# The residual add of block 11 as an accumulating DMA on the GpSimd queue, in a cross-network kernel with a full TensorE

## Chip, cores, metric

One core of one Trainium2 chip. The metric is device time in microseconds. All runs quoted are marked fast, and repeated runs of the kernel before agree within 0.1%.

## The reference

Six layers of a "deep cross network" on 16384 rows of 1024 columns, in bf16:

```python
# x0: (16384, 1024), ws: (6, 1024, 1024), bs: (6, 1024)
x = x0
for l in range(6):
    proj = jnp.einsum('bd,de->be', x, ws[l]) + bs[l]
    x = x0 * proj + x
return x
```

## The kernel before

The batch is cut into 16 pairs of 2 x 512 rows; a pair goes through its six layers before the next starts. x lives in SBUF transposed, as four quadrants (half of the columns, half of the rows). The 2 x 2 block product is done with seven products instead of eight (sums T1 to T4 of x quadrants against precombined weights), and in pairs 1 to 15 two of the seven (5 and 2) are cut once more in the same way. The result of the blocks comes out of PSUM through ScalarE into Q (block 11), U, V, W; VectorE then adds the shared part, multiplies by x0 and adds into x. In pair 0 the kernel also makes the precombined weights; 36 copies on GpSimd's DMA queue store them in HBM (`Lc`), and these are the "GpSimd copies" of the prediction.

Every operation is put into a list with a rank, and a small list scheduler emits them in the order of rank as soon as their tags allow; the order on each engine is therefore fixed when the kernel is built. The parts that matter here (`#...` marks cuts):

```python
# weights: a ring of 16 buffers; SyncE loads ahead as far as TensorE has freed buffers
def pump():
    while pos["next"] < len(ring_seq):
        u, w, kind = ring_seq[pos["next"]]
        #...
        nc.sync.dma_start(t[:], w_src(units[u][1], w))
        pos["next"] += 1

# ranks of a middle layer, in microseconds from its start (cut)
#   5cc@10.88 T3@11.48 2cc@12.61 Q1@13.35 Qm@14.62 Qa@15.89 Ua@17.43 ... T1@-1.14

B11, B12, B21, B22 = blk(xs, 0, 0), blk(xs, 0, 1), blk(xs, 1, 0), blk(xs, 1, 1)
ttop("T1", T[1][:], B12, B11, SUB, [XI[0, 1], XI[0, 0]], ["T1"])      # first reader of the new x11
ttop("T2", T[2][:], B22, T[1][:], SUB, [XI[1, 1], "T1"], ["T2"])
ttop("T3", T[3][:], B22, B12, SUB, [XI[1, 1], XI[0, 1]], ["T3"])
#...
group(f"P1.{m}", "1", pA[m], A[m], B11, [XI[0, 0]], m, True)          # first matmuls that read x11
#...
ttop("Q1", Q[:], Q[:], P1s[:], ADD, allm("Q") + allm("P1s"), allm("Q"))
for nm, C, q in (("Q", Q, (0, 0)), ("U", U, (0, 1)), ("V", V, (1, 1)), ("W", W, (1, 0))):
    #...
    ttop(nm + "m", C[:], C[:], blk(x0T, *q), MULT, ...)               # Qm, Um, Vm
    ttop(nm + ("a" if nm == "Q" else "x"), blk(xst, *q), C[:], blk(xs, *q), ADD, ...)  # Qa, Ux, Vx, Wx
#...
if l == (2 if pr == 0 else 0) and nxt < NPAIR:                        # next pair's x0, transposed on load
    #...
        op(base + 23 + n, ld, [], XN)
```

## Time and profile before

| | before |
|---|---|
| time | 2276.61 us (2276.53 to 2276.68) |
| TensorE / VectorE / ScalarE / GpSimd busy | 100% / 91% / 81% / 1% |
| one layer of pairs 1 to 15 | 23.45 us |
| DMA engines: SyncE's queue / GpSimd's queue | 79.1% / 2.2% of 16 engines |

Busy shares say how full an engine is, not whether it holds up the end. That is read from the chain that ended last and from who waits for whom; both are in the prediction. In the lines of a timeline the columns are start, duration, engine, source line, operation, written tile <- read tiles, shapes, count; a bracket gives the idle time just before and what ended it. `ev` are the buffers Q, U, V, W; `T` the sums T1 to T4; `ti` the inputs of the inner products; `xst` is x. "Landing" is the time from the start of a DMA's issuing instruction to the moment when its data is reported as written. The DMA share adds up the times of all packets and divides by the time of 16 engines; packets overlap, so it can exceed 1.

### The profile page before, as it was taken

Reading aid. Unit: us, or ns where it says so; the run is one execution under the profiler, and the core shown is the slowest. Engines: PE = TensorE matmul, PEld = TensorE weight load, DVE = VectorE, ACT = ScalarE, POOL = GpSimd, SP = SyncE. Lnnn points to the kernel's source line nnn. Section 1 sums busy time; section 2 is a strip of 40 time slices with the busy share of each in tenths; the row PEclk is TensorE's granted clock in tenths of the full one; section 3 lists DMA queues with packets and bytes.
Section 4 is the critical chain, followed back from the end, with each engine's and each line's share of the span. In section 5 each row is a group of like instructions: output and inputs, shape, how many; then the busy total and the mean of one; then the engine's idle time right before and its main releaser. Section 6 shows DMA issues by size and latency. Waiting matters only on the chain.

```text
span 2275.2 us, 34978 instructions
## 1 busy us (share of the span) xinstructions
PE 2265.4 (100%) x12951; PEld 1264.0 (56%) x12951; DVE 2079.9 (91%) x2326; ACT 1839.4 (81%) x3228; POOL 22.1 (1%) x43
## 2 busy tenths in 40 slices
PE   9999999999999999999999999999999999999998
PEld 4455555555555555555555555555555555555554
DVE  7999999999999999999999999999999999999997
ACT  5678888888888888888888888888888888888887
POOL 1110000000000000000000000000000000000000
PEclk9999999999999999999999999999999999999999
DMA  9779797796977969779697796978969689696872
GB/s 279 229 270 289 261 242 269 219 301 209 252 257 221 288 217 260 250 226 283 213 274 241 228 283 204 273 245 230 283 200 292 226 232 286 194 303 216 241 240 65
DMA packets 625868, 557.01 MB, mean 245 GB/s; under 512 B 397600, under 2 KB 552224, under 8 KB 625696
## 3 DMA queue, kind: packets, MB, share of 16 engines
q1 hardware_dynamic: 618864, 534.58, 79.1%
q0 software_dynamic: 5184, 18.88, 2.2%
q8 instruction: 101, 1.65, 0.3%
q10 hardware_dynamic: 1648, 1.32, 0.2%
q14 instruction: 71, 0.58, 0.1%
HBM read 436.22 MB, written 52.43 MB: 215 GB/s over the span
## 4 chain that ended last, share of the span: by engine, by line
PE 98%; DVE 1%; SPq 0%; DMA 0%; issue 0%; ACT 0%; DVEq 0%
PE pA L285 57%; PE pX L389 24%; PE pX L285 16%; DVE ev L198 1%; SPq L529 0%; DMA wp<-in_ws_dram 0%; DVE xst L198 0%; DVE T L198 0%; DVE ti L198 0%; DVE wp L198 0%; SPq L538 0%; ACT ev L294 0%; DVE x0T L487 0%; DVEq L608 0%; DVEq L198 0%
## 5 line engine op out<-in xcount | busy, mean ns | idle before, releaser
L285 PEld LDWEIGHTS <-wp 128*128 128x128 bf16 x7904 | 772.3, 98 | 843.7 <-issue 3.9
L285 PE MATMUL pA<-T,wp 128*128 128x512 bf16 x4608 | 1054.9, 379 | 0.5 <-DVE T L198 0.5
L294 ACT ACTIVATE ev<-pA,b_all 128x512 bf16<-128x512 f32 x1124 | 704.8, 690 | 211.8 <-PE pA L285 211.4
L389 PEld LDWEIGHTS <-wp 128*128 128x128 bf16 x4984 | 487.1, 98 | 156.6 <-issue 15.2
L198 DVE TENSOR_TENSOR ev<-ev,x0T 128x2048 bf16<-128x2048 bf16 (+2 forms) x484 | 482.7, 999 | 8.1 <-ACT ev L294 1.5
L198 DVE TENSOR_TENSOR xst<-ev,xst 128x2048 bf16<-128x2048 bf16 x319 | 388.9, 1219 | 18.6 <-DVE ev L198 0.5
L389 PE MATMUL pX<-ti,wp 128*128 128x256 bf16 x2848 | 397.6, 272 | 0.0
L198 DVE TENSOR_TENSOR ev<-ev,ev 128x2048 bf16<-128x2048 bf16 (+1 forms) x283 | 343.7, 1215 | 26.7 <-ACT ev L294 9.8
L294 ACT ACTIVATE ev<-pX,b_all 128x512 bf16<-128x512 f32 x412 | 289.4, 705 | 59.9 <-PE pX L285 49.3
L285 PE MATMUL pX<-xst,wp 128*128 128x512 bf16 x1376 | 336.4, 379 | 0.0
L285 PE MATMUL pA<-xst,wp 128*128 128x512 bf16 x1280 | 313.5, 379 | 0.0
L290 ACT COPY pX<-pA 128x512 f32<-128x512 f32 x412 | 256.3, 625 | 44.7 <-PE pA L285 44.3
L290 ACT CAST ev<-pX 128x512 bf16<-128x512 f32 x384 | 224.8, 619 | 49.0 <-ACT ev L294 37.6
L198 DVE TENSOR_TENSOR ev<-iu,ip 128x1024 bf16<-128x1024 bf16 x178 | 122.4, 688 | 120.7 <-ACT iu L290 120.7
L290 ACT COPY pX<-pX 128x512 f32<-128x512 f32 x356 | 208.7, 587 | 8.4
L290 ACT CAST iu<-pX 128x512 bf16<-128x512 f32 x356 | 196.8, 639 | 0.0
L198 DVE TENSOR_TENSOR T<-xst 128x2048 bf16<-128x2048 bf16 x160 | 194.8, 1217 | 0.3
L198 DVE TENSOR_TENSOR T<-xst,T 128x2048 bf16<-128x2048 bf16 x160 | 194.5, 1216 | 0.0
L389 PE MATMUL pX<-T,wp 128*128 128x256 bf16 x1068 | 160.2, 273 | 0.0
L290 ACT CAST ip<-pX 128x512 bf16<-128x512 f32 x178 | 104.7, 589 | 54.1 <-PE pX L389 54.1
L389 PE MATMUL pX<-xst,wp 128*128 128x256 bf16 x888 | 133.2, 273 | 0.0
L198 DVE TENSOR_TENSOR xst<-ev,x0T 128x2048 bf16<-128x2048 bf16 x64 | 78.2, 1222 | 1.6
(44 smaller groups left out, 624.3 us busy)
## 6 DMA issues: line engine op xcount, KB each, us to landing
wp<-Lc SPq DMA_DIRECT2D x538, 512.0 KB, 4.6
wp<-in_ws_dram SPq DMA_DIRECT2D x285, 512.0 KB, 5.3
out_dram<-x0T SPq DMA_DIRECT2D x30, 1024.0 KB, 8.6
Lc<-wp POOLq DMA_DIRECT2D x24, 512.0 KB, 6.2
Lc<-isum POOLq DMA_DIRECT2D x12, 512.0 KB, 6.9
w<-in_ws_dram SPq DMA_DIRECT2D x5, 512.0 KB, 6.3
wp<-in_ws_dram ACTq DMA_DIRECT2D x2, 512.0 KB, 5.8
out_dram<-x0T SPq DMA_DIRECT2D x2, 512.0 KB, 3.6
```

Of the source, the lines that this page charges most:

```text
L198: nc.vector.tensor_tensor(out=o, in0=a, in1=b, op=op)
L285: nc.tensor.matmul(bank[:], lhsT=wt[(u, w)][:, k, m * P:(m + 1) * P], rhs=rhs[:, k, :], start=(start and k == 0), stop=(k == KH - 1), skip ...
L290: add(name, lambda: nc.scalar.copy(out=dst, in_=src), rd, wr)
L294: add(name, lambda: nc.scalar.activation(out=dst, in_=src, func=IDENT, bias=b_all[:, c:c + 1], scale=1.0), rd, wr)
L389: nc.tensor.matmul(pX[bank][:, m * NQ:(m + 1) * NQ], lhsT=wv[:, k, m * P:(m + 1) * P], rhs=rhs[:, k, :], start=(start and m == 0 and k == ...
```

## The change

VectorE is the second fullest engine and GpSimd does nothing after pair 0. The intent is to take one of VectorE's large adds away: from layer 1 of pair 1 on (in layer 0 the sum is written to another buffer, so there is nothing to accumulate into), Q is added into x by a DMA that reads Q and x and writes x.

```diff
                     ttop(nm + "m", C[:], C[:], blk(x0T, *q), MULT, allm(nm) + [X0[q]], allm(nm))
+                if nm == "Q" and l > 0 and not one:
+                    add("Qa", lambda C=C, q=q, xst=xst: nc.gpsimd.dma_start(out=blk(xst, *q), in_=C[:], accum_op=ADD), allm(nm) + [XI[q]], [XO[q]])
+                    continue
                 ttop(nm + ("a" if nm == "Q" else "x"), blk(xst, *q), C[:], blk(xs, *q), ADD, allm(nm) + [XI[q]], [XO[q]])
```

## The prediction

> **What bounds the kernel now.** I read the page from the top: busy shares, chain, DMA queues, then the timeline of two engines in a middle layer, then the DMA load of four stretches.
>
> ```profile
> PE 2265.4 (100%) x12951; PEld 1264.0 (56%) x12951; DVE 2079.9 (91%) x2326; ACT 1839.4 (81%) x3228; POOL 22.1 (1%) x43
> q1 hardware_dynamic: 618864, 534.58, 79.1%
> q0 software_dynamic: 5184, 18.88, 2.2%
> PE 98%; DVE 1%; SPq 0%; DMA 0%; issue 0%; ACT 0%; DVEq 0%
> L198 DVE TENSOR_TENSOR xst<-ev,xst 128x2048 bf16<-128x2048 bf16 x319 | 388.9, 1219 | 18.6 <-DVE ev L198 0.5
> ```
>
> TensorE never stops: 100% busy at a granted clock of 0.999, and 98% of the chain that ended last is TensorE. VectorE is second at 91%, but TensorE's waits for it are fractions of a microsecond in the whole run. So taking work off VectorE cannot shorten anything; the change can only be neutral or put a new wait in front of TensorE. The question is whether the add, done by DMA, is ready when it is needed. The block-11 product Q, the sum into x, and the next user of x stand so in a middle layer (VectorE first, TensorE after; the eleven matmul lines between are left out):
>
> ```profile
> 1060.83 1.22 DVE L198 TENSOR_TENSOR ev<-ev,x0T 128x2048 bf16<-128x2048 bf16 x1
> 1062.15 1.23 DVE L198 TENSOR_TENSOR xst<-ev,xst 128x2048 bf16<-128x2048 bf16 x1
> 1063.46 1.23 DVE L198 TENSOR_TENSOR ev<-ev,ev 128x2048 bf16<-128x2048 bf16 x1
> ...
> 1068.26 1.22 DVE L198 TENSOR_TENSOR T<-xst 128x2048 bf16<-128x2048 bf16 x1
> 1069.40 0.68 DVE L198 TENSOR_TENSOR ev<-ev,x0T 128x1024 bf16<-128x1024 bf16 x1
> 1070.00 0.68 DVE L198 TENSOR_TENSOR ti<-T 128x1024 bf16<-128x1024 bf16 x1
> ...
> 1069.45 1.89 PE L285 MATMUL pA<-xst,wp 128*128 128x512 bf16 x8
> 1071.17 0.60 PE L389 MATMUL pX<-ti,wp 128*128 128x256 bf16 x4
> ```
>
> The first line is the multiplication by x0 (Qm), the second the add that the change removes (Qa), the third the next block's first add (Ua), then T1 = B12 - B11, the first reader of the new x; the first two TensorE groups of the next layer read x and then a product of T1.
>
> **The window.** Qm ends at 1060.83 + 1.22 = 1062.05. T1 starts at 1068.26: 6.2 us later. Beyond that there is almost no slack. From T1 on VectorE works without a gap, and T2 = B22 - T1 ends just in time: in the layer before, T2 ran from 1052.96 to 1054.18 and its matmuls began at 1054.26, 0.08 us later. The inner-product input made from T1 ends at 1070.68, its matmuls start at 1071.17, 0.5 us later. So the DMA is free if it lands within about 6.3 us of Qm's end; each microsecond beyond delays T1, T2 and TensorE, and through TensorE the next layer's Q. TensorE has no idle time in which to make it good. The layer is a loop (T1, inner products, Q1, Qm, DMA, T1), so an excess counts once per layer.
>
> **What the Trainium skill says.** "DMA: Bandwidth & Descriptors", section "SWDGE vs HWDGE vs iDMA", ties accumulation during a DMA to the software descriptor path from GpSimd, so the queue is not a choice. The same page, "Issuing engines are not separate DMA queues", says transfers from all issuers interleave on the same 16 DMA engines; a separate queue buys no bandwidth. The trace agrees in kind: the 36 GpSimd copies of pair 0 land in anything from 3.0 to 11.4 us, by what else is in flight. "Collectives: The Full Stack", section on the bandwidth ceiling ("why AG ≠ RS ≠ AR"), says that a DMA add needs two source reads through one read ring and so gets half the rate of a copy; no run here shows it yet. "SBUF — State Buffer", section "Who interferes with whom", says that tensor_tensor has no two-port mode and so should not hold up descriptor writing. The trace agrees: the 36 issues on GpSimd all took 531 to 670 ns although VectorE was busy nearly all the time beside them.
>
> **The change part by part.** *Removed:* the instruction order shows 74 VectorE instructions fewer (2318 to 2244 rows): pairs 1 to 14 five each, pair 15 four (its last layer has its own code). 74 x 1.22 us = 90 us of VectorE work; its share would fall from 91% to about 87%. Worth on the path: nothing. In the layer above, Ua waits for ScalarE's U, which TensorE paces, so with Qa gone VectorE idles some 1.3 us and Ua starts where it did.
>
> *Moved:* nothing of weight. The matmul order, the ScalarE order and the SyncE order are the same but for line numbers; the VectorE order lacks Qa.
>
> *Added:* 74 accumulating DMAs of 512 KB (128 rows of 4 KB), 0.53 us of GpSimd issue each, on an engine that is idle by then. Fourteen of them (layer 5) have no tight reader, since the next layer reads another pair's x0. 60 are on the path: layers 1 to 4 of 15 pairs.
>
> Their DMA cost: the 36 copies on this queue took 2.2% of 16 engines' span, 0.022 x 2275.2 / 36 = 1.39 us of all engines each. With two reads, I estimate 2.6 us (1.39 doubled, less something for overlap). 74 x 2.6 = 190 us, 8% of the span, on top of 82%: still below saturation on average, so weights should keep coming. They are prefetched through 16 ring buffers, and in the queue's own waits SyncE spent over 1300 us waiting for TensorE to free a buffer, so there is a long lead.
>
> Latency is what matters, and there the stages differ. The window of 6.2 us after Qm in layers 1, 2, 3, 4 of one pair (last columns: granted clock, DMA share, GB/s):
>
> ```profile
> 1038.60:1044.80 6.20, 6.20 (x31) 2.83 (x29) 5.94 (x6) 3.94 (x7) 0.00 (x0) 1.00 1.20 224
> 1062.10:1068.30 6.20, 6.20 (x30) 2.84 (x29) 5.99 (x6) 3.94 (x7) 0.00 (x0) 1.00 1.04 376
> 1085.50:1091.70 6.20, 6.20 (x31) 2.84 (x29) 5.95 (x5) 3.94 (x7) 0.00 (x0) 1.00 0.74 227
> 1109.00:1115.20 6.20, 6.20 (x30) 2.84 (x29) 6.00 (x6) 3.94 (x7) 0.00 (x0) 1.00 0.76 222
> ```
>
> All other pairs that I looked at show the same pattern: saturated in layer 1 (transposes of the next pair's x0 and of the last result) and layer 2 (weights catching up), about 0.7 in 3 and 4. GpSimd copies of pair 0 at similar loads, by issue time and time to landing (the first two with their stretch):
>
> ```profile
> 82.40:91.70 9.30, 9.30 (x45) 4.22 (x44) 9.23 (x10) 6.38 (x12) 0.97 (x2) 1.00 1.20 215
> ...
> DMA to landing us min/median/max: 9.3/9.3/9.3
> ...
> 115.50:118.50 3.00, 3.00 (x15) 1.37 (x14) 3.00 (x3) 1.66 (x3) 0.51 (x1) 1.00 0.75 306
> ...
> DMA to landing us min/median/max: 3.0/3.0/3.0
> ```
>
> Others: 6.8 to 8.5 us where weights saturated the engines (issues at 145, 157, 162 us), 3.0 to 5.3 us at shares of 0.6 to 0.8. For the second read I add 1.2 us in a free and up to 2 us in a full stage. Estimates of landing and excess over 6.3 us:
> - layer 1: about 10.3 us, excess 4.0; x15 = 60 us;
> - layer 2: about 8.3 us (copies of 6.8 to 8.5, less than full addition because a stall in layer 1 lets the backlog drain and SBUF, not HBM, is the target), excess 2.0; x15 = 30 us;
> - layers 3 and 4: about 5.7 us, mostly hidden; a mean excess of 0.2; x30 = 6 us.
>
> Sum 96 us. I take a fifth off, since these rest on copies to HBM and on single samples: 78 us, so 2276.6 + 78 = 2355 us.
>
> **The rivals.** (a) *All hidden, 2277 us.* For it: copies land in 3.0 us in free stages, SBUF as target may be quicker, and the window is 6.3 us. Against: two of four critical layers have full DMA engines. If layer 1 alone overshoots by 2 us, the cost is 30 us, +1.3%: within 2%. (b) *The DMA add is far slower than two reads,* because the adder in the DMA engine or small pieces set its pace: landing at 12 us everywhere would be 60 x 5.7 = 340 us, 2620 us. No line of the profile speaks for it, none excludes it. (c) *Weights become the bound:* the added traffic pushes back loads in the saturated layers. Against: TensorE never waits for a DMA of weights now, and the ring runs ahead. Worth 0 to 30 us. (d) *Faster*: would need TensorE to have idle time that VectorE causes; it has none.
>
> **Range and chances.** Low end 2278, where the transfers are hidden; high end 2440, where layers 3 and 4 overshoot by about 2 us too (60 us more) and layer 1 a little more. Faster by over 2%: 0.01. Within 2% (up to 2322 us): 0.29, for rival (a) and its near misses. Slower: 0.70.
>
> **What would show it.** VectorE near 87% busy and 74 fewer adds into x. A new idle line of T1's instruction waiting for the DMA into x, tens of microseconds in sum, mostly in layers 1 and 2, near zero in 3 and 4, and TensorE waiting for x or T about as long. If landings are under 6.3 us in all layers, rival (a) holds; if over 9 us in layers 3 and 4, rival (b); if TensorE waits for weights instead, rival (c). The queue's share tells the second read: from 36 copies at 1.39 us to 74 more at 2.6 or so.

## The result

| | before | after |
|---|---|---|
| time (median) | 2276.61 us | 2429.06 us (2418.74 and 2439.39) |
| ratio | | 1.067 (95%: 1.059 to 1.075) |

Ratios here and below are the mean time of one kernel's fast runs over that of the other's of the same rounds, so not quite the ratio of the medians. The change costs 152 us in the medians. The profiled execution of the changed kernel took 2437.6 us against 2275.2 before: 162.4 us to be explained in the trace.

The head of the page after, with busy shares, two DMA queues, the chain by engine and by line, and the groups that now wait:

```profile
PE 2308.5 (95%) x12951; PEld 1263.6 (52%) x12951; DVE 1995.0 (82%) x2252; ACT 1841.8 (76%) x3228; POOL 86.5 (4%) x117
q1 hardware_dynamic: 618864, 534.58, 74.4%
q0 software_dynamic: 15840, 57.68, 10.5%
PE 55%; DMA 20%; DVE 13%; ACT 10%; issue 2%; SPq 0%; DVEq 0%; POOLq 0%; ACTq 0%
L285 PE MATMUL pA<-xst,wp 128*128 128x512 bf16 x1280 | 324.4, 389 | 87.9 <-DMA xst<-ev 83.9
L198 DVE TENSOR_TENSOR T<-xst 128x2048 bf16<-128x2048 bf16 x160 | 195.4, 1221 | 157.4 <-DMA xst<-ev 156.9
L198 DVE TENSOR_TENSOR xst<-ev,xst 128x2048 bf16<-128x2048 bf16 (+1 forms) x245 | 298.4, 1218 | 10.7
L435 POOL DMA_DIRECT2D xst<-ev x74 | 64.3, 870 | 2171.7 <-DVE ev L198 1264.7
xst<-ev POOLq DMA_DIRECT2D x74, 512.0 KB, 8.2
```

TensorE was the whole chain; now a fifth of it is the DMA into x. VectorE has its 74 adds fewer (319 to 245) and 85 us less work, and none of that shows in the time: with the adds gone and nothing in their place (run 11 below) VectorE's waits for ScalarE's `ev` rise from 11.4 to 114.9 us, as the prediction had it. Instead T1 on VectorE waits 156.9 us for the DMA and the first matmuls on x 83.9 us; the two waits run side by side, so they are not added. The last line is the one to look at: the median DMA lands 8.2 us after its issue.

The chain of waits through one layer 3 of the changed kernel (start, duration, what), from the multiplication Qm to the next layer's first inner product:

```profile
1028.99 1.24 DVE ev L198
1030.23 0.03 POOLq L435
1030.26 0.49 issue
1030.75 8.03 DMA xst<-ev
1038.78 0.03 issue
1038.81 0.05 DVEq L198
1038.86 0.04 issue
1038.90 1.23 DVE T L198
1040.13 0.60 DVE ev L198
1040.73 0.61 DVE ti L198
1041.35 0.04 issue
1041.39 0.61 PE pX L389 x4
```

Qm ends at 1030.23, the DMA is issued half a microsecond later, lands 8.03 us after that, and T1 starts at 1038.90: 8.7 us after Qm, where it was 6.2 us before. The timeline shows what the two engines did meanwhile:

```profile
1035.45 1.22 DVE L198 TENSOR_TENSOR ev<-ev,ev 128x2048 bf16<-128x2048 bf16 x1
1038.90 1.23 DVE L198 TENSOR_TENSOR T<-xst 128x2048 bf16<-128x2048 bf16 x1 [2.23 <-DMA xst<-ev]
...
1038.92 1.89 PE L285 MATMUL pA<-xst,wp 128*128 128x512 bf16 x8 [0.97 <-DMA xst<-ev]
1041.39 0.60 PE L389 MATMUL pX<-ti,wp 128*128 128x256 bf16 x4 [0.58 <-DVE ti L198]
```

**By layer.** The issue times of the 74 DMAs give the length of each layer: the distance from one issue to the next, less 23.45 us (two layers after layer 5, since layer 0 has none), is what that DMA cost.

| layer of the DMA | landing, median (range) | lost, sum | mean of one |
|---|---|---|---|
| 1 | 8.3 us (5.8 to 16.4) | 48.7 us | 3.2 us |
| 2 | 8.6 us (7.1 to 9.5) | 43.2 us | 2.9 us |
| 3 | 8.3 us (7.7 to 8.7) | 36.1 us | 2.4 us |
| 4 | 8.1 us (4.5 to 8.8) | 32.5 us | 2.3 us |
| 5 (no tight reader) | 8.1 us (7.8 to 9.2) | 2.3 us | 0.16 us |

The sum is 162.8 us, the whole difference. In layer 1 the worst DMA stalled TensorE for 9.5 us, and the clock came down too: the granted clock was 0.84 and 0.86 in the two stretches of 17 us from 1254 us on, against 1.00 in the same stretches before. It is not the only such place: in the profiled execution the granted clock was 0.5 in seven stretches of 3.4 to 10.2 us, each around or just after a wait of TensorE of 2.1 to 9.5 us in layers 1 and 2 (`--windows 1265.6:1275.8` shows one). TensorE was busy for 27.5 us of them, so I estimate that some 14 of the 162 us are slower matmuls and not waiting. With the DMA in layers 3 and 4 alone (run 9 below) no stretch but the last 2 us of the run has such a clock. Layer 5 is a control inside the run: the same DMAs land as late and cost nothing. The single 4.5 us is the run's last DMA: no packet of another queue runs beside it.

### The profile page after: what moved, and what is told of

It reads as the page before. It is cut to its first block, busy times and chain, and to the rows that moved or that the text cites. A ratio compares the mean times of both kernels' runs of the same rounds, so it can differ in the third digit from the quotient of the medians.

```text
span 2437.6 us, 35012 instructions
## 1 busy us (share of the span) xinstructions
PE 2308.5 (95%) x12951; PEld 1263.6 (52%) x12951; DVE 1995.0 (82%) x2252; ACT 1841.8 (76%) x3228; POOL 86.5 (4%) x117
## 3 DMA queue, kind: packets, MB, share of 16 engines
q0 software_dynamic: 15840, 57.68, 10.5%
## 4 chain that ended last, share of the span: by engine, by line
PE 55%; DMA 20%; DVE 13%; ACT 10%; issue 2%; SPq 0%; DVEq 0%; POOLq 0%; ACTq 0%
PE pA L285 29%; DMA xst<-ev 19%; PE pX L389 17%; PE pX L285 9%; DVE ev L198 6%; ACT ev L294 3%; DVE T L198 3%; ACT iu L290 2%; ACT ev L290 2%; DVE ti L198 2%; ACT pX L290 2%; DVE xst L198 2%; DMA wp<-Lc 1%; SPq L532 0%; DMA wp<-in_ws_dram 0%
## 5 line engine op out<-in xcount | busy, mean ns | idle before, releaser
L285 PE MATMUL pA<-xst,wp 128*128 128x512 bf16 x1280 | 324.4, 389 | 87.9 <-DMA xst<-ev 83.9
L198 DVE TENSOR_TENSOR T<-xst 128x2048 bf16<-128x2048 bf16 x160 | 195.4, 1221 | 157.4 <-DMA xst<-ev 156.9
L198 DVE TENSOR_TENSOR xst<-ev,xst 128x2048 bf16<-128x2048 bf16 (+1 forms) x245 | 298.4, 1218 | 10.7
L290 ACT COPY pX<-pA 128x512 f32<-128x512 f32 x412 | 248.3, 605 | 44.8 <-PE pA L285 44.4
L435 POOL DMA_DIRECT2D xst<-ev x74 | 64.3, 870 | 2171.7 <-DVE ev L198 1264.7
```

The lines of the kernel that those rows point to most:

```text
L198: nc.vector.tensor_tensor(out=o, in0=a, in1=b, op=op)
L285: nc.tensor.matmul(bank[:], lhsT=wt[(u, w)][:, k, m * P:(m + 1) * P], rhs=rhs[:, k, :], start=(start and k == 0), stop=(k == KH - 1), skip ...
L290: add(name, lambda: nc.scalar.copy(out=dst, in_=src), rd, wr)
L435: add("Qa", lambda C=C, q=q, xst=xst: nc.gpsimd.dma_start(out=blk(xst, *q), in_=C[:], accum_op=ADD), allm(nm) + [XI[q]], [XO[q]])
```

## The experiments

The numbers follow the argument. Names such as `e4_fewload` are the runs' labels.

Theory A: the loss is the wait for the landing (with the slower clock that goes with the long waits), and nothing else. Theory B: it is the added traffic (starved weight loads, or slower engines). Within A it was open what makes a landing of 8 us: the second read, the sharing with weight loads, the software queue itself, or the transposing loads.

**1. Same traffic, no wait.** (`e1_spare`)

```diff
-  nc.gpsimd.dma_start(out=blk(xst, *q), in_=C[:], accum_op=ADD) ... continue
+  nc.gpsimd.dma_start(out=isum[0][:], in_=C[:], accum_op=ADD)   # a buffer that is free after pair 0
+  # no continue: VectorE still adds Q into x
```

> The 74 accumulating DMAs stay, with the same source, size and issue point, but add into a spare SBUF buffer, and VectorE keeps the add into x: the traffic without the wait. Theory A (the lost time is TensorE and VectorE waiting for the landing, about 8.2 us against a window of 6.3 us): 2277 to 2285 us, and no wait for these DMAs; landings still about 8 us. Theory B (the 206 us of extra DMA engine time starves the weight loads, or the traffic slows the engines): 2350 us or more, with TensorE waiting for weights.

Measured: 2277.82 us, ratio 1.0002 (0.9987 to 1.0017), correct. The DMAs landed as late as in the changed kernel (earlier in layer 1 alone, a median of 6.4 us against 8.3), with nobody waiting:

```profile
q0 software_dynamic: 15840, 57.68, 11.2%
isum<-ev POOLq DMA_DIRECT2D x74, 512.0 KB, 8.0
```

The 74 DMAs cost nothing as traffic. Theory B falls: weights come in time with the queues at 11.2% and 79.5%.

**2. A copy in place of the add** (`e2_copy`; wrong result): `accum_op=ADD` removed.

> Wrong result on purpose: a plain copy of the product into x on the same queue in place of the accumulating DMA, nothing else changed. If the second read is what makes the landing late (own engine time 2.64 us to about 1.35 us, and less sharing with the weight loads on top), landings fall from 8.2 to about 6 us and the time to 2280 to 2320 us. If the landing is mostly fixed cost of the software queue or waiting for its turn, landings stay above 7 us and the time above 2360 us.

Measured: 2329.80 us, ratio 1.0228 (1.0204 to 1.0251). The queue's share fell to 6.6%; landings in layers 3 and 4 had medians of 6.4 and 6.5 us, and one such DMA cost 0.62 and 0.72 us. So adding instead of copying is worth 1.6 to 1.9 us of landing there and about 100 us of time, but even a plain copy would not have been hidden. That the cause is the second read is argued, not shown: the packet records count 144 packets and 512 KB for a copy and an add alike, and an adder at half speed would look the same. The time is 10 us above the expected range: the landings were 0.4 us longer than I had thought.

**3. Fewer weight loads** (`e4_fewload`; wrong result): in pairs 1 to 15 the blocks 6, 3, 7 and 4 use resident buffers.

```diff
+            if kind == "load" and units[u][0] > 0 and w in ("6", "3", "7", "4"):
+                wt[(u, w)] = isum[("6", "3", "7", "4").index(w)]
+                pos["next"] += 1
+                continue
```

> Wrong result on purpose: from pair 1 on four of the nine weight blocks of a layer (6, 3, 7, 4) are not loaded; the matmuls read resident buffers. DMA traffic by weights falls to 5/9; the accumulating DMAs are unchanged. If sharing the engines with the weight loads makes up some 2.5 to 3.5 us of the 8.2 us in layers 3 and 4, landings there fall to 5 to 6.5 us and the time to 2280 to 2330 us. If the landing is a property of the accumulating DMA itself, it stays near 8 us and the time near 2420 us.

Measured: 2336.93 us, ratio 1.026 (1.0234 to 1.0287): by the total, a miss. By layer it is the clearest run of all. The issues on GpSimd in layers 1 to 5 of one pair (start, duration; the time between them is a layer):

```profile
339.61 0.86 POOL L439 DMA_DIRECT2D xst<-ev  x1 [46.13 <-ACT ev L298]
368.06 0.86 POOL L439 DMA_DIRECT2D xst<-ev  x1 [27.59 <-ACT ev L298]
391.51 0.87 POOL L439 DMA_DIRECT2D xst<-ev  x1 [22.59 <-ACT ev L298]
414.97 0.87 POOL L439 DMA_DIRECT2D xst<-ev  x1 [22.58 <-ACT ev L298]
438.42 0.87 POOL L439 DMA_DIRECT2D xst<-ev  x1 [22.58 <-ACT ev L298]
```

From the second issue on the layers are 23.45, 23.46 and 23.45 us long, as without any DMA; over the whole run layers 3 and 4 lost 0.2 and 0.3 us in sum, with landings of 4.5 us. So 3.6 to 3.8 us of the 8.1 to 8.3 us in these layers is sharing with the weight loads. All the remaining loss, 49.8 us, lies in layer 1 (28.45 us in the lines), where landings have a median of 9.3 us. With fewer weights ahead of them in SyncE's queue the transposing loads of the next pair's x0 mostly start 10 to 13 us ahead of that DMA (in the changed kernel 5 to 6 us) and are in full flow when it is issued. I had not thought of that.

**4. Are the transposing loads the cause in layer 1?** (`e8_few_trmove`) As run 3, with these loads moved from layer 0's rank to layer 4's (wrong result).

```diff
-        if l == (2 if pr == 0 else 0) and nxt < NPAIR:
+        if l == (2 if pr == 0 else 4) and nxt < NPAIR:
-                op(base + 23 + n, ld, [], XN)
+                op(base + (23 if pr == 0 else 9) + n, ld, [], XN)
```

> Wrong result on purpose: as e4_fewload (four weight blocks not loaded), and the transposing loads of the next pair's x0 moved from the start of layer 1 to the end of layer 4, so that they meet the DMA of layer 5, which has no tight reader. In e4_fewload layers 2 to 5 landed in 4.5 us and cost nothing, and layer 1 alone cost 50 us. If the transposing loads are the cause in layer 1: landing there falls to about 4.5 to 5 us and the time to 2277 to 2290 us. If layer 1 is late for another reason (the output transposes and stores of the last pair), it stays at 2320 us or more.

Measured: 2342.35 us, ratio 1.0271 (1.0236 to 1.0305). Taken by its total this would be the rival's number, but I had misjudged where the loads would start: SyncE issued them 7.7 us ahead of the DMA of layer 4, not of layer 5. By layer: layer 1 fell from 49.8 to 4.0 us lost (landing 4.6 us), and layer 4 rose from 0.3 to 60.7 us (landing median 8.8, up to 14.6 us). Everything else stayed. The loss went with the loads; the output transposes and stores, which stayed in place, are not the cause. The start alone does not decide how late a DMA gets: with the same 7.7 us in all 14 pairs, landings ran from 5.8 to 14.6 us. In the changed kernel the three latest DMAs of layer 1 were those beside which SyncE got both loads out in 10.5 to 10.6 us, and the three earliest (5.8 us) those beside which it took 12.3 to 13.1 us: the two give way to one another. The record also shows what tells the early from the late ones: which of the two loads SyncE was on when the DMA was issued. In the changed kernel and runs 1, 4, 5 and 10, SyncE was still issuing the first load beside 26 DMAs, and all of these landed in 5.7 to 6.8 us; beside 41 it had gone on to the second, and 38 of these took more than 7.5 us, up to 16.4 (the other three 6.4 to 6.9). In run 4, 12 of the 13 late ones landed within 0.3 us of that second load. Run 7 has one exception (8.2 us with the first load still being issued). Why the second load holds the DMA up stays open.

**5. The same move in the changed kernel** (`e9_trmove`; correct result).

> Correct result: the changed kernel with only the transposing loads of x0 moved from layer 1 to the end of layer 4. Their part in the loss is the outliers of layer 1 (48.7 us there now against about 35 us in layers 3 and 4) and the catching up of weights in layer 2 (43.2 us): some 15 to 25 us less, 2395 to 2425 us. If layers 1 to 4 alike stay 2.3 us late each, the floor is 2277 + 60 x 2.35 = 2418 us.

Measured: 2449.69 us, ratio 1.0755 (1.0739 to 1.0771): a miss in the wrong direction. Layers 1 to 4 lost 46.8, 32.4, 35.4 and 54.1 us. Layer 2 improved by 11 us, layer 4 got the outliers (landings up to 14.7 us), and layer 1 hardly improved: without the loads of x0 its window is full of weight loads (a DMA share of 1.07 on average in the 6.2 us after the issue).

**6. Half of it by DMA** (`e3_half`), the other half by VectorE (correct result).

```diff
-  nc.gpsimd.dma_start(out=blk(xst, *q), in_=C[:], accum_op=ADD)
+  nc.gpsimd.dma_start(out=blk(xst, *q)[:, 0:KQ], in_=C[:, 0:KQ], accum_op=ADD)
+  tt(blk(xst, *q)[:, KQ:KH], C[:, KQ:KH], blk(xst, *q)[:, KQ:KH], ADD)      # VectorE
```

> The DMA adds only the first half of the block (256 KB), VectorE adds the other half: correct result. With half the bytes the DMA's own time falls from 2.64 to about 1.35 us of all engines, and its sharing with the weights by a bit less than half. From the copy run (6.3 us with the same own time) landings of about 6.2 us in layers 3 and 4, 0.5 us over the limit of about 5.7 us counted from the issue: 2300 to 2335 us. If two reads cost more than their bytes (more packets, more turns), landings stay above 7 us and the time above 2360 us.

Measured: 2348.63 us, ratio 1.0313 (1.0298 to 1.0328). The queue's share (6.8%) is that of the copy, but landings in layers 3 and 4 have medians of 7.1 and 7.0 us, 0.5 to 0.7 us more than the copy's. Half the bytes save only some 1.1 us of landing. Most of the difference from the copy is there without the weights too: the last DMA of each run, with next to nothing beside it, landed in 3.29 us (half add), 2.84 us (copy) and 4.49 us (full add). Of the 0.45 us, the longer issue on GpSimd, 0.87 us against 0.54, could make up 0.33; that was not varied by itself, and neither was the size of the packets (as many, of half the size).

**7. An earlier issue?** (`e5_t3late`) VectorE does T3 after Qm instead of before it.

```diff
-  T3 at rank 11.48 (ahead of 2cc, Q1, Qm)
+  T3 at rank 14.7  (after Qm at 14.62)
```

> Same DMAs, but VectorE does T3 after Qm and not before it, so Qm ends and the DMA issues some 1.1 us earlier in the layer. Theory A: each of the 60 critical layers gets 1.1 us back, 60 x 1.1 = 66 us: about 2360 us (2340 to 2375). Theory B: no change, about 2425 us. If T3 late makes TensorE wait for block 7, slower than expected by up to 20 us.

Measured: 2456.36 us, ratio 1.0766 (1.0716 to 1.0817), so slower than the changed kernel: both theories' numbers missed. VectorE in one layer of this run:

```profile
1968.77 0.69 DVE L198 TENSOR_TENSOR ev<-iu,ip 128x1024 bf16<-128x1024 bf16 x1 [0.28 <-ACT iu L290]
1970.34 1.23 DVE L198 TENSOR_TENSOR ev<-ev,ev 128x2048 bf16<-128x2048 bf16 x1 [0.88 <-ACT ev L290]
1971.60 1.23 DVE L198 TENSOR_TENSOR ev<-ev,x0T 128x2048 bf16<-128x2048 bf16 x1
1972.74 1.22 DVE L198 TENSOR_TENSOR T<-xst 128x2048 bf16<-128x2048 bf16 x1
```

The time that T3 left free is spent waiting for ScalarE, which still moves Q out of PSUM (0.88 us before Q1). Q is not late because of VectorE's order, so the premise was false for this move; and T3, now late, holds up block 7: TensorE waited for a T 88 times, 38.0 us in sum, against 0.4 us in the changed kernel. This move does not widen the window; no other was tried.

**8. Only where nobody waits** (`e6_layer5`): the DMA add in layer 5 alone (`l == L - 1`), 14 DMAs, correct result.

> The DMA add only in layer 5 of pairs 1 to 14 (14 DMAs), where the next layer starts on another pair's x0 and nobody needs the sum soon; VectorE adds in all other layers. Theory A: hidden, 2277 to 2280 us. A rival, that each software DMA costs something by being there (descriptor traffic, issue, output transposes held up), would give 14 x 2 us or more: above 2300 us.

Measured: 2277.71 us, ratio 0.9999 (0.9984 to 1.0013). As Theory A has it.

**9. Layers 3 and 4 alone** (`e10_l34`; `l in (3, 4)`), where the prediction had the DMA hidden; correct result.

> Correct result: the DMA add only in layers 3 and 4 (30 DMAs), where the prediction had it hidden. From the trace of the changed kernel 30 x 2.3 us: 2340 to 2350 us. If their lateness comes only from what layers 1 and 2 leave behind in the queues, it vanishes here: 2277 to 2290 us, as predicted at first.

Measured: 2345.79 us, ratio 1.0301 (1.0286 to 1.0317): 68 us. The lateness there is their own, not a leftover of layers 1 and 2.

**10. Layers 1 and 2 alone** (`e11_l12`; `l in (1, 2)`); correct result.

> Correct result: the DMA add only in layers 1 and 2 (30 DMAs). From the trace of the changed kernel 49 + 43 = 92 us: about 2368 us (2350 to 2385, since layer 1 scatters). Together with the layers 3 and 4 run the two losses should add up to that of the changed kernel, about 152 us; if the stalls help one another's queues to drain, they add up to more.

Measured: 2352.50 us, ratio 1.0329 (1.0277 to 1.0382): 75 us (range of runs 65 to 90). With the 68 us of run 9 that makes 143 us, against 152 us for the whole change: they add up within the scatter of layer 1.

**11. What the change could gain at most** (`e7_noadd`): the 74 adds dropped, nothing in their place.

```diff
-                    add("Qa", lambda ...: nc.gpsimd.dma_start(...), ...)
                     continue
```

> Wrong result on purpose: the 74 adds are dropped and nothing takes their place; neither VectorE nor a DMA does them. This is the most that taking them off VectorE could be worth. If TensorE sets the pace: 2277 us as before, VectorE near 87%. If VectorE's 91% costs anything: 2270 us or less.

Measured: 2277.33 us, ratio 1.0 (0.9985 to 1.0015), VectorE at 87%:

```profile
PE 2265.3 (100%) x12951; PEld 1264.3 (56%) x12951; DVE 1989.3 (87%) x2252; ACT 1839.4 (81%) x3228; POOL 22.1 (1%) x43
```

Taking 90 us off VectorE is worth nothing even if the replacement is free. (The comparison with the reference passed this run as correct although a term is missing, presumably because this term is too small beside x for its tolerance. So "correct" says little about this add in the other runs either; run 2, which overwrites x with the term, was caught.)

No version beats the kernel before. Runs 1, 8 and 11 reach its time, and run 11 shows that this is all there is to reach by taking this add off VectorE.

## Why the prediction came out as it did

The direction, the cause and the range held: slower, by a wait of T1 and TensorE for the landing, 2429 us within 2278 to 2440. The predicted cost was 78 us and the measured one 152 us, so about half of it was missing. The high end of the range had been put where "layers 3 and 4 overshoot by about 2 us too", and this is what happened (2.3 to 2.4 us each); with a timed run at 2439.39 us it held by little. Step by step:

- **TensorE bounds, VectorE's relief is worth nothing: right**, and now shown by run 11.
- **The limit, "within about 6.3 us of Qm's end": right.** It can be checked from three runs. Landing (median, from the issue) less the mean loss of a DMA, in layers 3 and 4: copy 6.4 - 0.62 and 6.5 - 0.72, half 7.1 - 1.29 and 7.0 - 1.21, full 8.3 - 2.41 and 8.1 - 2.32. All six give 5.8 to 5.9 us. From Qm's end to the issue there is another 0.5 us (the chain above), and the sum is 6.3 us. The half microsecond itself I had left out: my landings were counted from the issue and compared with a limit counted from Qm. That mistake is worth about 15 us in the prediction's own sum: 30 DMAs of layers 1 and 2, each 0.5 us later. In layers 3 and 4 the 5.7 us it assumed would still have been just inside.
- **"an excess counts once per layer": right.** The six differences above agree, and runs 9 and 10 add up.
- **DMA time of one add, 2.6 us: nearly right.** 10.5% of 2437.6 us is 256 us; less 36 copies at 1.39 us (50 us) and over 74 that is 2.8 us, twice a copy. In layers 3 and 4 alone it is 2.6 us, against 1.3 us for the copy of run 2. So the engine time agrees with the "half the rate of a copy" that the prediction took from the skill, though that passage speaks of the reduce step of a collective. The landing alone does not double (4.49 us against 2.84), and whether the second read is the reason was not separated from the adder.
- **"layers 3 and 4: about 5.7 us, mostly hidden": wrong, and the step that made the forecast too low.** They landed at 8.1 to 8.3 us and cost 69 us in the trace, not 6. I took the DMA share of 0.74 in the window for mostly free engines and used copies at similar shares as the model. Run 3 shows what the share hid: the weight loads beside it are worth 3.6 to 3.8 us. In such a window the engines are not free for a quarter of a transfer; they are shared as long as both have work: in the 8.2 us that an add of layer 3 takes to land, its own packets use 2.6 us of all engines and SyncE's queue 5.0 us, while the copy's 6.4 us hold 1.3 and 4.6 us.
- **Layer 2, 8.3 us and 30 us: mis-sized by little.** 8.6 us and 43 us; of the 13 us, 15 x 0.5 = 8 us is the issue gap.
- **Layer 1, 10.3 us and 60 us: about right in sum (49 us), wrong in shape.** I had expected every DMA there to be late. A third landed within 6.3 us, and three took 11.9, 14.5 and 16.4 us. Run 4 shows that the transposing loads make the late ones; the late ones are those issued after SyncE had gone on to the second load, and why is open. This scatter is probably why the two timed runs of the changed kernel differ by 21 us: the runs of experiment 10, with layer 1, spread over 25 us, those of experiment 9, without it, over 5 us.
- **"I take a fifth off": wrong.** The reasons given for it did not hold: SBUF as target was hardly quicker (the lone copy of run 2 took 2.84 us, the quickest copies to HBM 2.96 and 3.04 us). The uncorrected sum of 96 us was nearer.
- **Rivals.** (a) hidden: refuted by the trace. (b) an adder that sets the pace: its landing of 12 us everywhere is refuted, since a lone DMA lands in 4.5 us; a smaller part of the adder in the 2.6 us is not excluded. (c) weights as the new bound: refuted by run 1, and in the changed kernel itself TensorE waits 0.6 us in all for a weight load.

## What to carry to other kernels

Before moving work from one engine to a DMA, subtract the end of the producer from the start of the first consumer, take off the issue gap (0.5 us here), and compare what is left with the landing time under load, not with the transfer's own time: here 2.8 us of transfer was 8 us of latency. If a kernel is full on one engine and the moved work was not on that engine's chain, drop the work first (run 11), since that shows the most there is to gain in one run. When a total refutes a theory, look at the parts before giving it up: runs 3 and 4 missed their totals and yet showed two causes, the weight loads in layers 2 to 4 (run 3) and the transposing loads in layer 1 (run 4).

## What the Trainium skill lacked or had wrong

- "DMA: Bandwidth & Descriptors" ("SWDGE vs HWDGE vs iDMA") says who can accumulate but has no figure for it. Here an SBUF to SBUF accumulate of 512 KB keeps GpSimd 0.87 us per issue (a copy 0.53 to 0.54 us), costs 2.8 us of all 16 engines on average, lands in 4.5 us alone and in 8.1 to 8.3 us beside weight loads.
- The same page ("Anatomy of one DMA") fits a GpSimd DMA as 2.0 us plus the bytes over 436 GB/s, which gives an estimate of 3.2 us for 512 KB. Alone the copy of run 2 took 2.8 us (one sample), close to it; beside weight loads 6.4 us, and next to transposing loads up to 12.3 us. The page says that transfers interleave on the same engines, but has no figure for how landing grows when they do.
